# A threshold moved to ScalarE, value products regrouped, and gMLP one step later, in an attention and gMLP kernel

## The chip, the cores and the metric

The kernel runs on one core of a Trainium2 chip. The time is device microseconds of one execution. The kernel before was run three times: 563.73, 563.22 and 558.63 us, median 563.22. A further execution was recorded by the hardware profiler: its own time is 562.84 us, and the span from its first to its last instruction is 561.1 us. All rows of the profile come from that execution.

The engines are named as the profile names them: PE (TensorE, matmuls; PEld its weight loads), DVE (VectorE), ACT (ScalarE), POOL (GpSimd) and SP (SyncE, which here only issues DMAs). An issue queue has a q behind its name: SPq.

## The reference

For 8 batches of 8 heads, 576 positions and 64 values per head, each row of scores is thresholded: what lies more than tau (0.02) under the row's maximum is dropped before the softmax. The joined heads then go through a gMLP block, in which `w_spatial` mixes positions.

```python
scores = scale * np.matmul(q, k.transpose(0, 1, 3, 2))
thresh = np.max(scores, axis=-1, keepdims=True) - tau
scores = np.where(scores >= thresh, scores, -1000000000.0)
scores = scores - np.max(scores, axis=-1, keepdims=True)
attn = np.exp(scores)
attn = attn / (np.sum(attn, axis=-1, keepdims=True) + 1e-09)
x = np.matmul(attn, v)                      # heads joined: (8, 576, 512)

h = np.maximum(x @ w_in, 0.0)
u, v = h[..., :512], h[..., 512:]
v_n = (v - mean(v)) / np.sqrt(var(v) + 1e-06)          # over the last axis
v_s = np.einsum('ts,bsd->btd', w_spatial, v_n) + b_spatial[None, :, None]
out = (u * v_s) @ w_out
```

## The kernel before

**Pairs and steps.** Two heads of a batch make a pair; there are 32 pairs, four to a batch. The 576 query rows of a pair are cut into four chunks of 128 for each head and one remainder chunk, in which the last 64 rows of both heads share the 128 partitions. A step handles one chunk: step `g` is pair `g // 5`, chunk `c = g % 5`. So a batch is 20 steps, and the pairs are 160 steps. The order of all instructions is written out by hand: every engine works through its own instructions in program order, and DMAs go out in program order on the queue that issues them, nearly all on SP's.

**A step** (`step`, line 478) issues, in this order: the score matmuls of its chunk into one of two score tiles in PSUM (`scores`, lines 445 and 448); evictions held over from the step before; the first of up to two jobs; the row maximum on DVE, negated (`negm`, line 491); the eviction of the first job, if DVE does it; `e = exp(s - max)` on ACT, one activation per head (line 499); then `mask`, for the chunk of the step before; then what stands in the list `sends`; then second parts of the v jobs; then the second job. Jobs that ACT evicts come ahead of those that DVE evicts. If the second job is one that ACT evicts, its eviction is held until the next step begins. Jobs write to two one-bank tiles in PSUM, named f, in turn.

**mask** (line 459) makes `p = e * (e >= exp(-tau))` on DVE. Chunks 0 and 1 share a tile, as do 2 and 3; after the second of the two, one DMA on SP's queue transposes both into `pT`. The remainder chunk has its own, smaller operation (`pr`, line 473) and its own transpose into `ptr` (line 476). Since `mask` runs a step late, the remainder's is issued in step 0 of the next pair.

**Value products** (`pv`, line 251) of a pair run in steps 3 and 4 of the next pair, one head each: for each of five chunks, five matmuls of 65 columns add up over the keys. The 65th column of the value tile is one, so it gives the row sum. DVE evicts with a reciprocal (line 274) and a multiply (line 275) into `xn`. After the second head, the transpose of `xn` into `xT` is put into `sends`, which SP issues (line 281); with four of them the batch is ready for gMLP.

**gMLP jobs.** Each batch has 20: five each of v (line 308; relu on ACT at line 333, a square with a sum on ACT at line 341, the normalizing on POOL), u (lines 359 and 364; relu on ACT), s (lines 389 and 394, the product with `w_spatial`; DVE multiplies by u into `gT`) and o (line 418, the product with `w_out`; ACT copies, SP sends it out). `ORDER` gives the job of each of the 20 steps that begin 27 steps after the batch's first step; an `o` there belongs to the batch before. In the first three steps of a pair, the other job transposes the next pair's q and k on PE (lines 226 and 239), with a copy by ACT. What falls behind the last pair's steps is in a list of its own (`last`).

**w_spatial.** Between steps 23 and 35 POOL casts its five row chunks (`shape_ws`, line 182), each followed at once by a transposing DMA on SP's queue into `wsT` (line 189). In step 37, three small DMAs put the bias rows into the same tile (line 202).

Of the kernel before, what the change touches and what calls it, by code (L numbers as in the profile page):

```python
# [8 lines left out]
F32 = mybir.dt.float32  # L9
BF16 = mybir.dt.bfloat16  # L10
AX = mybir.AxisListType
ALU = mybir.AluOpType
ACT = mybir.ActivationFunctionType
# [4 lines left out]
def kernel(  # L18
# [16 lines left out]
    nc = tc.nc  # L35
    B, H, S, D = q.shape
# [5 lines left out]
    P = 128  # L42
# [5 lines left out]
    small = ctx.enter_context(tc.tile_pool(name="small", bufs=6))  # L48
# [11 lines left out]
    ctau = const.tile([P, 1], F32, name="ctau")  # L60
# [4 lines left out]
    pr_ring = [const.tile([P, 640], BF16, name=f"pr{i}") for i in range(2)]  # L65
# [34 lines left out]
    wsT = const.tile([P, 5, 640], BF16, name="wsT")  # L100
    wsb = const.tile([P, 5, 640], BF16, name="wsb")


    def load(i, n, w, eng=nc.sync):

        b, hp = divmod(i, HP)
        t = ld_ring[i // 2 % 2][w][:, 2 * (i % 2):2 * (i % 2) + 2 * n]
        src = (q, k, v)[w][b, 2 * hp:2 * hp + 2 * n]

        def main():  # L110
            eng.dma_start(
                out=t[:, :, 0:4, :],
                in_=src[:, 0:512, :].rearrange("h (p c) d -> p h (c d)", c=4))

        def rest():
            eng.dma_start(out=t[0:64, :, 4, :],
                          in_=src[:, 512:576, :].rearrange("h p d -> p h d"))

        def rest_b():
            nc.sync.dma_start(  # L120
                out=vx_ring[i // 2 % 2][64:128],
                in_=src.rearrange("(j h) s d -> h s j d", h=2)[1, 512:576])
        return [main, rest] + ([rest_b] if w == 2 else [])
# [32 lines left out]
    bias = mw.tile([P, 2, S], F32, name="gT")  # L156
# [25 lines left out]
    def shape_ws(c):  # L182
        n = P if c < 4 else 64
        src = wsl[c // 2][:n, c % 2, :]
        nc.gpsimd.tensor_copy(
            out=wsb[:n, c, 0:512].rearrange("p (sc sp) -> p sc sp", sc=4),
            in_=src[:, 0:512].rearrange("p (sp sc) -> p sc sp", sc=4))
        nc.gpsimd.tensor_copy(out=wsb[:n, c, 512:576], in_=src[:, 512:576])
        nc.sync.dma_start_transpose(out=wsT[:, :, c * P:(c + 1) * P], in_=wsb[:, c, :])

    def shape_bias(_):

# [14 lines left out]
    def bank():  # L207

        banks[0] += 1
        if "scores" in done_with and banks[0] % 2:  # L210
            return ps_s.tile([P, 1536], F32, name="s")[:, 0:512]
        return ps_f.tile([P, 512], F32, name="f")

    done_with = set()
    sends = []
    qks, pts, xns, xts = {}, {}, {}, {}

    def qk_main(i, which):
# [29 lines left out]
            nc.gpsimd.tensor_copy(out=kd[64:128, 64:128], in_=qks[i][64:128, 1, 512:576])  # L248
        return "act", mm, ev

    def pv(i, h):
        b, hp = divmod(i, HP)
        hold = {}
        vt = v_ring[i % 4]

        def mm():
            t = hold["t"] = bank()
            for c in range(5):
                for j in range(5):
                    if c < 4:  # L260
                        lhs = pts[i, c // 2][:, c % 2, 4 + (j + 1) % 5 if h else j, :]
                        rhs = vt[:, (10 if j == 4 else 5 + j) if h else j, :]
                    else:
                        lhs = pts[i, 2][:, j, 64 * h:64 * h + P]
                        rhs = vt[:, 5 * h + j, :]
                    nc.tensor.matmul(out=t[:, c * 65:c * 65 + 65], lhsT=lhs, rhs=rhs,  # L266
                                     start=(j == 0), stop=(j == 4))

        def ev():
            o = hold["t"][:, 0:325].rearrange("p (c d) -> p c d", d=65)  # L270
            if h == 0:
                xns[i] = xp.tile([P, 5, P], BF16, name="xn")
            r = small.tile([P, 5], F32, name="r")
            nc.vector.reciprocal(out=r, in_=o[:, :, 64])
            nc.vector.tensor_tensor(out=xns[i][:, :, h * D:(h + 1) * D], in0=o[:, :, 0:64],  # L275
                                    in1=r.unsqueeze(2).broadcast_to([P, 5, 64]), op=ALU.mult)
            if h == 1:
                if hp == 0:
                    xts[b] = xtp.tile([P, 4, 640], BF16, name="xT")
                xn = xns[i]  # L280
                sends.append(lambda: nc.sync.dma_start_transpose(
                    out=xts[b][:, hp, :].rearrange("p (c s) -> p c s", s=P),
                    in_=xn.rearrange("p c d -> p (c d)")))
        return "dve", mm, ev

    us, gs = {}, {}
# [149 lines left out]
    def scores(i, c):  # L436


        s = ps_s.tile([P, 1536], F32, name="s")
        qk = qks[i]  # L440

        def mm(h, out, lo, n):
            hs = slice(64 * h, 64 * h + 64)
            m = slice(c * P, min((c + 1) * P, S))
            return nc.tensor.matmul(out=out, lhsT=qk[hs, 0, m], rhs=qk[hs, 1, lo:lo + n],  # L445
                                    start=True, stop=True)
        if c < 4:
            nc.tensor.matmul(out=view(s, 512, [[448, 2], [1, 64]]),  # L448
                             lhsT=qk[:, 0, c * P:(c + 1) * P], rhs=kd_ring[i % 2],
                             start=True, stop=True)  # L450
            mm(0, s[:, 0:512], 0, 512)
            mm(1, s[:, 1024:1536], 0, 512)
            return view(s, 0, [[960, 2], [1, S]])
        for lo, off in ((0, 224), (288, 512)):
            for h in range(2):
                mm(h, s[64 * h:64 * h + 64, off:off + 288], lo, 288)
        return s[:, 224:800].rearrange("p (h s) -> p h s", h=1)

    def mask():
        i, c, e = unmasked.pop()  # L460
        if c < 4:
            pt = p_ring[c // 2]
            ef = e.rearrange("p h s -> p (h s)")
            nc.vector.scalar_tensor_tensor(out=pt[:, c % 2, :], in0=ef, scalar=ctau, in1=ef,  # L464
                                           op0=ALU.is_ge, op1=ALU.mult)
            if c % 2:
                dst = ptp.tile([P, 2, 9, P], BF16, name="pT")
                nc.sync.dma_start_transpose(out=dst.rearrange("p c b s -> p (c b) s"),
                                            in_=pt.rearrange("p c s -> p (c s)"))
                pts[i, c // 2] = dst  # L470
        else:
            pt = pr_ring[i % 2]
            nc.vector.scalar_tensor_tensor(out=pt[:, 0:S], in0=e[:, 0, :], scalar=ctau,  # L473
                                           in1=e[:, 0, :], op0=ALU.is_ge, op1=ALU.mult)
            pts[i, 2] = ptr_ring[i % 3]
            nc.sync.dma_start_transpose(out=pts[i, 2][:, :, 0:P], in_=pt)

    def step(i, c, f1, f2):

        if i is not None:  # L480
            s = scores(i, c)
        while held:
            held.pop(0)()
        if f1:
            f1[1]()
            if f1[0] == "act":
                f1[2]()
        if i is not None:
            nh = 2 if c < 4 else 1
            nm = small.tile([P, 2], F32, name="negm")  # L490
            nc.vector.tensor_reduce(out=nm[:, 0:nh], in_=s, axis=AX.X, op=ALU.max, negate=True)  # L491
        if f1 and f1[0] == "dve":
            f1[2]()
        due = [f for n, f in later if n <= 0]
        later[:] = [(n - 1, f) for n, f in later if n > 0]
        if i is not None:
            e = ep.tile([P, 2, S], F32, name="e")
            for h in range(nh):
                nc.scalar.activation(out=e[:, h, :], in_=s[:, h, :], func=ACT.Exp,  # L499
                                     bias=nm[:, h:h + 1])  # L500
        ready = sends[:]
        sends.clear()
        if unmasked:
            mask()
        for f in ready:
            f()
        if i is not None:
            unmasked.append((i, c, e))
        for f in due:
            f()  # L510
        if f2:
            f2[1]()
            if f2[0] == "dve":
                f2[2]()
            else:
                held.append(f2[2])
# [7 lines left out]


    LAG = 27
    ORDER = "vuvvuvuvuu" + "oososososs"
    jobs = {}
    for b in range(B - 1):
        n = dict.fromkeys("vuso", 0)  # L530
        for j, t in enumerate(ORDER):
            f = {"v": moe_v, "u": moe_u, "s": moe_s, "o": moe_o}[t]
# [11 lines left out]
    with tc.manual_schedule():  # L544
# [23 lines left out]
        for g in range(5 * NPAIR + (len(last) + 1) // 2):  # L568
            slot, c = divmod(g, 5)
            i = slot if slot < NPAIR else None  # L570
# [65 lines left out]
```

## Time and profile before

| | us |
|---|---|
| median of three runs | 563.22 (558.63 to 563.73) |
| profiled execution | 562.84 |
| its span | 561.1 |
| PE busy in the span | 487.0 (87%) |
| DVE busy | 470.5 (84%) |
| ACT busy | 328.2 (59%) |
| POOL busy | 240.8 (43%) |
| granted TensorE clock, mean | 0.959 |

Busy times are sums over instructions and can lie beside each other. In a row of instruction groups come line, engine and operation, output and inputs, the shapes, the count, then busy us and the mean ns of one, then the engine's idle time just before them and what ended it. In a timeline row come the start, the duration, the engine, the line and the operation; a bracket gives the idle time before it and what released it. The granted clock is that of TensorE, in parts of full speed.

### The profile page before, as it was taken

The numbers are of one execution on the slowest core, as the hardware profiler recorded it, in microseconds if no ns is written. First come the engines' busy times: TensorE is split into PE (matmuls) and PEld (weight loads), VectorE is DVE, ScalarE is ACT, GpSimd is POOL, SyncE is SP. The second block draws the span as 40 slices with busy tenths as digits, with TensorE's granted clock in tenths as the row PEclk, the third lists the DMA queues.
The fourth block names the chain that finished last, engine by engine and source line by source line (L and its number), as shares of the span: only waits on it lengthen the run. The fifth ranks groups of instructions, "written<-read, shape, count | busy, mean of one in ns | idle before, by whom it ended". The sixth has DMA issues, their size and how long they took to land.

```text
span 561.1 us, 10240 instructions
## 1 busy us (share of the span) xinstructions
PE 487.0 (87%) x3848; PEld 257.7 (46%) x3848; DVE 470.5 (84%) x535; ACT 328.2 (59%) x609; POOL 240.8 (43%) x413
## 2 busy tenths in 40 slices
PE   6774887987898999899879999889989999989886
PEld 4342443544354555455435554445444554545433
DVE  3894988997898899889968999889987899989553
ACT  2553454774467755676546765677555766677241
POOL 5426622685407732377204752178303762064020
PEclk9896888997999999999999999999998999999989
DMA  8599797985987888968997698978987588755822
GB/s 235 107 214 185 140 207 134 217 146 125 208 173 158 180 182 184 195 94 224 166 174 145 127 217 150 189 141 165 205 187 157 98 198 188 119 107 102 192 65 84
DMA packets 243601, 90.91 MB, mean 162 GB/s; under 512 B 213024, under 2 KB 238112, under 8 KB 243552
## 3 DMA queue, kind: packets, MB, share of 16 engines
q1 hardware_dynamic: 241936, 88.39, 76.9%
q0 software_dynamic: 1200, 1.58, 2.3%
q8 instruction: 30, 0.49, 0.4%
q10 hardware_dynamic: 416, 0.30, 0.2%
q14 instruction: 19, 0.16, 0.1%
HBM read 33.31 MB, written 9.44 MB: 76 GB/s over the span
## 4 chain that ended last, share of the span: by engine, by line
PE 47%; DVE 24%; DMA 12%; ACT 10%; issue 5%; SPq 1%; POOL 0%; ACTq 0%; POOLq 0%
PE s L445 18%; DVE negm L491 14%; PE f L266 7%; DVE p L464 7%; DMA ptr<-pr 7%; ACT e L499 5%; PE f L389 4%; DMA xT<-xn 4%; PE s L448 3%; PE f L359 3%; PE f L308 3%; PE f L418 3%; ACT sq L341 2%; DVE xn L275 1%; ACT vrel L333 1%
## 5 line engine op out<-in xcount | busy, mean ns | idle before, releaser
L499 ACT ACTIVATE e<-s,negm 128x576 f32<-128x576 f32 x288 | 199.5, 740 | 96.8 <-DVE negm L491 77.4
L491 DVE TENSOR_REDUCE negm<-s 128x2 f32<-128x1152 f32 (+1 forms) x160 | 197.2, 1233 | 47.3 <-PE s L445 45.9
L445 PE MATMUL s<-qkT 64*128 64x512 f32 (+1 forms) x768 | 191.1, 590 | 1.0 <-ACT e L499 1.0
L464 DVE SCALAR_TENSOR_TENSOR p<-e,ctau 128x1152 bf16<-128x1152 f32 x128 | 187.5, 1465 | 0.0
L445 PEld LDWEIGHTS s<-qkT 64*128 64x128 f32 (+1 forms) x768 | 55.6, 173 | 29.2 <-issue 2.8
L247 POOL COPY kd<-qkT 64x64 f32<-64x64 f32 x32 | 13.0, 406 | 129.4 <-ACT qkT L243 124.7
L230 ACT COPY qkT<-f 128x512 f32<-128x512 f32 x64 | 37.6, 588 | 50.1 <-PE f L226 50.1
L266 PEld LDWEIGHTS <-pT 128*128 128x128 bf16 x1280 | 49.1, 100 | 37.4 <-issue 25.8
L448 PE MATMUL s<-kd,qkT 128*128 128x128 f32 x256 | 55.4, 299 | 8.5 <-ACT e L499 5.5
L266 PE MATMUL f<-v,pT 128*128 128x65 bf16 x1260 | 53.1, 197 | 9.0 <-ACT vrel L333 4.6
L448 PEld LDWEIGHTS s<-kd,qkT 128*128 128x128 f32 x256 | 45.5, 197 | 21.8 <-ACT e L499 8.8
L308 PE MATMUL f<-w_in,xT 128*128 128x512 bf16 x140 | 37.8, 387 | 11.0 <-DMA xT<-xn 9.5
L142 POOL COPY kn<-kl 128x640 f32<-128x640 f32 x32 | 26.1, 817 | 32.8 <-DMA kl<-in_k_dram 20.3
L389 PE MATMUL f<-wsT,vn 128*128 128x512 bf16 x150 | 38.0, 384 | 2.1 <-ACT o L426 1.6
L335 POOL TENSOR_SCALAR nmean<-sm 128x1 f32<-128x1 f32 x35 | 11.8, 338 | 64.8 <-ACT vrel L333 64.8
L266 PE MATMUL f<-v,ptr 128*128 128x65 bf16 x315 | 21.2, 199 | 19.2 <-DMA ptr<-pr 19.2
L359 PE MATMUL f<-xT,w_in 128*128 128x512 bf16 x120 | 32.6, 396 | 5.8 <-ACT vrel L333 5.8
L139 POOL TENSOR_SCALAR qn<-ql 128x640 f32<-128x640 f32 x32 | 30.5, 953 | 11.6 <-DMA ql<-in_q_dram 10.7
L418 PE MATMUL f<-w_o,gT 128*128 128x512 bf16 (+1 forms) x128 | 33.8, 388 | 0.5
L333 ACT ACTIVATE vrel<-f 128x512 f32<-128x512 f32 x35 | 20.8, 595 | 20.8 <-PE f L308 20.8
L275 DVE TENSOR_TENSOR xn<-f,r 128x320 bf16<-128x320 f32 x63 | 31.0, 491 | 2.2
L473 DVE SCALAR_TENSOR_TENSOR pr<-e,ctau 128x576 bf16<-128x576 f32 x32 | 31.9, 997 | 0.0
(101 smaller groups left out, 530.5 us busy)
## 6 DMA issues: line engine op xcount, KB each, us to landing
vl<-in_v_dram SPq DMA_DIRECT2D x16, 512.0 KB, 4.7
out_dram<-o SPq DMA_DIRECT2D x32, 256.0 KB, 2.7
ql<-in_q_dram SPq DMA_DIRECT2D x15, 512.0 KB, 4.5
kl<-in_k_dram SPq DMA_DIRECT2D x15, 512.0 KB, 4.6
uT<-in_moe_w_spatial_dram SPq DMA_DIRECT2D x2, 576.0 KB, 5.1
vl<-in_v_dram SPq DMA_DIRECT2D x16, 64.0 KB, 2.8
pT<-p SPq DMA_TRANSPOSE x64, 5.5
w_in<-in_moe_w_in_dram POOLq DMA_DIRECT2D x4, 256.0 KB, 5.7
```

The lines of the kernel that those rows point to most:

```text
L230: nc.scalar.copy(out=qks[i][:, which, 0:512], in_=hold["t"])
L266: nc.tensor.matmul(out=t[:, c * 65:c * 65 + 65], lhsT=lhs, rhs=rhs, start=(j == 0), stop=(j == 4))
L275: nc.vector.tensor_tensor(out=xns[i][:, :, h * D:(h + 1) * D], in0=o[:, :, 0:64], in1=r.unsqueeze(2).broadcast_to([P, 5, 64]), op=ALU.mult)
L308: nc.tensor.matmul(out=t, lhsT=xts[b][:, f, c * P:(c + 1) * P], rhs=w_in[:, f, 512:1024], start=(f == 0), stop=(f == 3))
L359: nc.tensor.matmul(out=t, lhsT=w_in[:, m, f * P:(f + 1) * P], rhs=xts[b][:, m, 0:512], start=(m == 0), stop=(m == 3))
L389: nc.tensor.matmul(out=t, lhsT=vn[:, c, f * P:(f + 1) * P], rhs=wsT[:, c, 0:512], start=(c == 0), stop=(c == 4))
L418: nc.tensor.matmul(out=t[:n], lhsT=gs[b][:, f, c * P:c * P + n], rhs=w_o[:, f, :], start=(f == 0), stop=(f == 3))
L445: return nc.tensor.matmul(out=out, lhsT=qk[hs, 0, m], rhs=qk[hs, 1, lo:lo + n], start=True, stop=True)
L448: nc.tensor.matmul(out=view(s, 512, [[448, 2], [1, 64]]), lhsT=qk[:, 0, c * P:(c + 1) * P], rhs=kd_ring[i % 2], start=True, stop=True)
L464: nc.vector.scalar_tensor_tensor(out=pt[:, c % 2, :], in0=ef, scalar=ctau, in1=ef, op0=ALU.is_ge, op1=ALU.mult)
L491: nc.vector.tensor_reduce(out=nm[:, 0:nh], in_=s, axis=AX.X, op=ALU.max, negate=True)
L499: nc.scalar.activation(out=e[:, h, :], in_=s[:, h, :], func=ACT.Exp, bias=nm[:, h:h + 1])
```

## The change

Four edits:

- The remainder chunk's threshold leaves DVE. In step c = 4, DVE adds tau to the negated maximum (one column). ACT then applies a parametric ReLU to `score - max + tau`: values from 0 on pass, values below are multiplied by 1e30. A second activation takes the exponential, written straight into the tile that is transposed. Dropped values become zero, kept ones lie between 1 and exp(tau); the common factor goes out with the row sum. The multiply with comparison in `mask` is gone for this chunk; the transpose is issued where it was.
- The value products are cut by chunks instead of heads: step 3 has chunks 0 and 1 of both heads, step 4 has chunks 2, 3 and the remainder of both.
- In `ORDER` the v and u jobs come one step later, and the first o of the batch before stands ahead of them. The s jobs and the other o jobs keep their places.
- The transposing send of each `w_spatial` chunk is put into `sends` twice over: the step's list only puts the real send into the list of the next step.

```diff
@@ shape_ws
-        nc.sync.dma_start_transpose(out=wsT[:, :, c * P:(c + 1) * P], in_=wsb[:, c, :])
+        sends.append(lambda: sends.append(lambda: nc.sync.dma_start_transpose(
+            out=wsT[:, :, c * P:(c + 1) * P], in_=wsb[:, c, :])))
@@ pv
-    def pv(i, h):
+    def pv(i, part):
+
         b, hp = divmod(i, HP)
         hold = {}
         vt = v_ring[i % 4]
+        c0, c1 = ((0, 2), (2, 5))[part]
+        w = 2 * (c1 - c0)
 
         def mm():
             t = hold["t"] = bank()
-            for c in range(5):
-                for j in range(5):
...
-                    nc.tensor.matmul(out=t[:, c * 65:c * 65 + 65], lhsT=lhs, rhs=rhs,
-                                     start=(j == 0), stop=(j == 4))
+            for c in range(c0, c1):
+                for h in range(2):
+                    at = (2 * (c - c0) + h) * 65
+                    for j in range(5):
+                        if c < 4:
+                            lhs = pts[i, c // 2][:, c % 2, 4 + (j + 1) % 5 if h else j, :]
+                            rhs = vt[:, (10 if j == 4 else 5 + j) if h else j, :]
+                        else:
+                            lhs = pts[i, 2][:, j, 64 * h:64 * h + P]
+                            rhs = vt[:, 5 * h + j, :]
+                        nc.tensor.matmul(out=t[:, at:at + 65], lhsT=lhs, rhs=rhs,
+                                         start=(j == 0), stop=(j == 4))
 
         def ev():
-            o = hold["t"][:, 0:325].rearrange("p (c d) -> p c d", d=65)
-            if h == 0:
+            o = hold["t"][:, 0:65 * w].rearrange("p (g d) -> p g d", d=65)
+            if part == 0:
                 xns[i] = xp.tile([P, 5, P], BF16, name="xn")
-            r = small.tile([P, 5], F32, name="r")
-            nc.vector.reciprocal(out=r, in_=o[:, :, 64])
-            nc.vector.tensor_tensor(out=xns[i][:, :, h * D:(h + 1) * D], in0=o[:, :, 0:64],
-                                    in1=r.unsqueeze(2).broadcast_to([P, 5, 64]), op=ALU.mult)
-            if h == 1:
+            xn = xns[i]
+            r = small.tile([P, 6], F32, name="r")
+            nc.vector.reciprocal(out=r[:, 0:w], in_=o[:, :, 64])
+            nc.vector.tensor_tensor(
+                out=xn[:, c0:c1, :].rearrange("p c (h d) -> p (c h) d", h=2),
+                in0=o[:, :, 0:64], in1=r[:, 0:w].unsqueeze(2).broadcast_to([P, w, 64]),
+                op=ALU.mult)
+            if part == 1:
...
@@ mask
         else:
-            pt = pr_ring[i % 2]
-            nc.vector.scalar_tensor_tensor(out=pt[:, 0:S], in0=e[:, 0, :], scalar=ctau,
-                                           in1=e[:, 0, :], op0=ALU.is_ge, op1=ALU.mult)
             pts[i, 2] = ptr_ring[i % 3]
-            nc.sync.dma_start_transpose(out=pts[i, 2][:, :, 0:P], in_=pt)
+            nc.sync.dma_start_transpose(out=pts[i, 2][:, :, 0:P], in_=pr_ring[i % 2])
@@ step
             e = ep.tile([P, 2, S], F32, name="e")
-            for h in range(nh):
+            if c == 4:
+
+                nc.vector.tensor_scalar_add(out=nm[:, 0:1], in0=nm[:, 0:1], scalar1=float(tau))
+                nc.scalar.activation(out=e[:, 0, :], in_=s[:, 0, :], func=ACT.Prelu,
+                                     bias=nm[:, 0:1], alpha=1e30)
+                nc.scalar.activation(out=pr_ring[i % 2][:, 0:S], in_=e[:, 0, :], func=ACT.Exp)
+            for h in range(2 if c < 4 else 0):
                 nc.scalar.activation(out=e[:, h, :], in_=s[:, h, :], func=ACT.Exp,
                                      bias=nm[:, h:h + 1])
@@
     LAG = 27
-    ORDER = "vuvvuvuvuu" + "oososososs"
+    ORDER = "ovuvvuvuvuuososososs"
```

More of the change, by code (lines that the diff above doesn't have):

```diff
@@ L101 @@
     wsb = const.tile([P, 5, 640], BF16, name="wsb")
+    sends = []
     def load(i, n, w, eng=nc.sync):
@@ L214 @@
     done_with = set()
-    sends = []
     qks, pts, xns, xts = {}, {}, {}, {}
@@ L254, in pv @@
         vt = v_ring[i % 4]
+        c0, c1 = ((0, 2), (2, 5))[part]
+        w = 2 * (c1 - c0)
         def mm():
             t = hold["t"] = bank()
-            for c in range(5):
-                for j in range(5):
[L260 to L266, printed above, removed]
-                                     start=(j == 0), stop=(j == 4))
+            for c in range(c0, c1):
[10 more added lines that the diff above has]
+                                         start=(j == 0), stop=(j == 4))
@@ L277, in ev @@
-            if h == 1:
+            xn = xns[i]
[6 more added lines that the diff above has]
+            if part == 1:
                 if hp == 0:
                     xts[b] = xtp.tile([P, 4, 640], BF16, name="xT")
-                xn = xns[i]
```

## The prediction

> **What bounds the kernel now.** I read four views, coarse to fine: the page's engine shares and its chain, busy times by stretch, the list of waits, and the timeline where the waits lie.
>
> ```profile
> PE 487.0 (87%) x3848; PEld 257.7 (46%) x3848; DVE 470.5 (84%) x535; ACT 328.2 (59%) x609; POOL 240.8 (43%) x413
> ...
> PE 47%; DVE 24%; DMA 12%; ACT 10%; issue 5%; SPq 1%; POOL 0%; ACTq 0%; POOLq 0%
> ```
>
> PE and DVE are nearly equal, and the chain changes between them, with DMA and ACT in between. So I cut the span: the start, the first batch, then five batches of gMLP, each 20 steps (four head pairs), cut at the same step. Columns: window, length, busy time of PE, PEld, DVE, ACT, POOL, granted clock, DMA share, GB/s.
>
> ```profile
> 30.00:107.00 77.00, 58.52 (x459) 30.93 (x458) 64.10 (x68) 37.16 (x63) 32.86 (x48) 0.87 0.94 182
> 107.00:170.29 63.29, 53.99 (x454) 29.16 (x452) 56.09 (x59) 37.70 (x71) 32.26 (x54) 0.95 0.85 169
> 170.29:233.34 63.05, 57.65 (x483) 31.04 (x482) 57.16 (x62) 41.24 (x79) 28.53 (x50) 1.00 0.83 176
> 233.34:300.39 67.05, 59.25 (x483) 31.50 (x482) 57.90 (x63) 41.24 (x79) 28.68 (x50) 0.97 0.87 168
> 300.39:363.42 63.03, 57.65 (x483) 31.02 (x482) 57.05 (x62) 41.24 (x79) 28.27 (x50) 1.00 0.89 164
> 363.42:429.49 66.07, 60.57 (x482) 32.37 (x482) 57.70 (x63) 41.33 (x79) 28.59 (x50) 0.95 0.85 173
> 429.49:490.75 61.26, 57.67 (x483) 31.13 (x482) 56.87 (x62) 41.23 (x79) 28.28 (x50) 1.00 0.72 150
> 490.75:520.00 29.25, 27.09 (x227) 14.02 (x227) 27.07 (x31) 21.76 (x44) 15.99 (x30) 1.00 0.57 111
> ```
>
> At clock 1.00 a batch holds 57.65 us of PE work. The five whole batches from 170 on last 64.1 on average, the best 61.26. What lies above 57.65 is PE's waits, and 1.6 to 2.9 us more matmul time where the clock fell. The start, 30 to 107, has DMA at 0.94: there the transfers are the limit, not an engine. Now by pairs, in the same columns:
>
> ```profile
> 395.55:412.00 16.45, 15.69 (x119) 8.16 (x118) 15.83 (x18) 9.57 (x16) 4.30 (x7) 1.00 0.91 170
> 412.00:430.60 18.60, 16.08 (x124) 8.37 (x123) 13.35 (x17) 9.63 (x19) 1.12 (x5) 0.82 0.77 178
> 430.60:446.37 15.77, 14.29 (x113) 7.62 (x114) 13.85 (x14) 12.15 (x26) 11.47 (x22) 1.00 0.55 103
> 446.37:461.63 15.26, 14.53 (x129) 8.22 (x130) 14.35 (x16) 9.98 (x18) 11.13 (x17) 1.00 0.87 200
> 461.63:477.60 15.97, 15.18 (x117) 7.96 (x116) 15.35 (x18) 9.10 (x16) 4.55 (x7) 1.00 0.77 178
> 477.60:491.86 14.26, 13.69 (x126) 7.32 (x125) 13.64 (x17) 10.01 (x19) 1.45 (x5) 1.00 0.70 118
> ```
>
> Three kinds of pair. The pair of s and o jobs (first and fifth row) is DVE's: 15.83 of 16.45. The v and u pairs (third, fourth) are PE's with ACT in the way. The pair in which a batch's v jobs begin (second and last) takes 14.26 or 18.60. The waits say why; columns are waiter, releaser, total us, times, longest.
>
> ```profile
> PE f L266 <- DMA ptr<-pr: 19.2, 10, 6.1
> ...
> PE f L308 <- DMA xT<-xn: 9.5, 5, 3.4
> ...
> PE f L359 <- ACT vrel L333: 5.8, 7, 0.8
> ...
> PE f L364 <- ACT uT L374: 4.5, 6, 0.8
> ```
>
> **The change part by part.**
>
> *Remainder threshold on ScalarE.* The prices:
>
> ```profile
> L499 ACT ACTIVATE e<-s,negm 128x576 f32<-128x576 f32 x288 | 199.5, 740 | 96.8 <-DVE negm L491 77.4 <-DVE r L274 18.6
> ...
> L473 DVE SCALAR_TENSOR_TENSOR pr<-e,ctau 128x576 bf16<-128x576 f32 x32 | 31.9, 997 | 0.0
> ...
> L323 DVE TENSOR_SCALAR rs<-mv 128x1 f32<-128x1 f32 x5 | 0.8, 154 | 0.2
> ```
>
> DVE loses 32 of 0.997 us and gains 32 single-column adds; the nearest row is 0.154, so 0.84 is saved per pair, 27.0 us in all. ACT gains one activation per pair, at most 0.740 by the row with the same shape and a column bias: 23.7 us, to 352 of 561. On the path, step c=4 has one more hop: negm, add, Prelu, and only then is the score bank free, 0.15 us later than now. Where the value products are that step's first job, the add stands on DVE behind their eviction, so Prelu (and on ACT behind it the next step's q and k copies) waits for that; this is so before gMLP starts and in one pair per batch. Between nothing (that bank is next wanted two steps on) and the eviction's own 0.7, I put 0.3 us per batch.
>
> The 0.84 us counts where DVE is last: in the s/o pair, and there only down to PE's own 15.69 of 16.45 or 15.18 of 15.97, so at most 0.8; I take 0.6. In the v/u pairs it falls into DVE's idle time; there ACT goes from 12.15 to 12.9 of 15.77, still below. Does an earlier pr bring ptr earlier?
>
> ```profile
> 429.63 2.75 SPq L468 DMA_TRANSPOSE pT<-p  x1
> ...
> 432.44 0.62 SPq L116 DMA_DIRECT2D vl<-in_v_dram  x1
> ...
> 433.15 1.26 SPq L476 DMA_TRANSPOSE ptr<-pr  x1
> ```
>
> Hardly: SP's queue goes from the transpose of p to a load to ptr with 0.1 us between. DVE's pr is covered by SP itself, so I give this nothing.
>
> *Value products by chunk groups.* Still 50 matmuls, two reciprocals and two multiplies over 640 columns per pair; the pieces are 4 and 6 groups for 5 and 5, so the work is unchanged. What moves is the need. Now the first head at c=3 wants all five chunks; after, c=3 wants chunks 0 and 1 only, and ptr is wanted by the last ten matmuls of c=4, one step (15.77/5 = 3.15 us) later. The longest wait:
>
> ```profile
> 48.65 1.24 SPq L476 DMA_TRANSPOSE ptr<-pr  x1
> ...
> 55.14 0.46 PE L266 MATMUL f<-v,ptr 128*128 128x65 bf16 x5 [6.11 <-DMA ptr<-pr]
> ```
>
> Here PE and behind it DVE stood still, and the scores of c=4 and the threshold of the chunk before stood behind them. With the need one step later about 3 of 6.11 remain; the waits under 3.8 go. But this one lies where DMA is at 0.94: 0.94 of 77 is 72.4 us of transfers, so that stretch can't go below about 73. I give it 3 of its 77 (bounds 0 and 5).
>
> *w_spatial sends delayed.* In 107 to 170:
>
> ```profile
> 127.85 1.20 SPq L189 DMA_TRANSPOSE wsT<-wsb  x1
> ...
> 129.77 2.10 SPq L476 DMA_TRANSPOSE ptr<-pr  x1
> ...
> 134.44 0.45 PE L266 MATMUL f<-v,ptr 128*128 128x65 bf16 x5 [3.76 <-DMA ptr<-pr]
> ```
> ```profile
> SPq L189 <- POOL nm L346: 4.4, 1, 4.4
> ```
>
> SP stood 4.4 us for POOL's cast of w_spatial, with ptr and xT queued behind, and PE then 3.76 for ptr. Sent from the next step's list, the transpose comes behind ptr. New: the last one goes out a step before the bias rows are placed in the same tile, and SP waits for its landing there, some 1.5 us; nothing needs it for two steps. With the later need of ptr I give this window 4.5 of its 9.3 us idle (63.29 less 53.99); bounds 2 and 6.
>
> *gMLP one step later.* The v and u jobs move on by a step, and the first o of the batch before takes the vacated place; s and the other o jobs stay, the tail too. In the pair of 18.60:
>
> ```profile
> 415.89 1.34 SPq L281 DMA_TRANSPOSE xT<-xn  x1
> ...
> 420.02 0.61 PE L308 MATMUL f<-w_in,xT 128*128 128x512 bf16 x1 [2.30 <-DMA xT<-xn]
> ```
>
> xT arrives at 420.0; v asked at 420.02 less 2.30, 417.7. After, PE does the o matmuls there (they need the last gT, as v's bank does now) and next step's scores first, so it asks about 2.5 us later: waits up to 3.4 shrink to under 1. With the wait goes the slow clock behind it: 16.08 of PE for 124 matmuls at 0.82, 13.69 for 126 at 1.00. The Trainium skill ("TensorE: Matmul & The Clock Gate", Part 1) says that the clock halves after an idle window of about 3.4 us; taken literally a wait of 2.30 would not do it, the clock loss would stay in two batches, and the sum would end near 540, inside the forecast's range. The trace shows the fall after the shorter wait, so by the row it goes with the wait.
>
> The moved v jobs also change who waits for ACT: in the v/u pairs the square stands on ACT ahead of the relu that frees PE's bank:
>
> ```profile
> 433.25 0.72 ACT L341 ACTIVATE sq<-vrel,nmean 128x512 bf16<-128x512 f32 x1
> ...
> 433.96 0.59 ACT L333 ACTIVATE vrel<-f 128x512 f32<-128x512 f32 x1
> ...
> 434.69 1.02 PE L359 MATMUL f<-xT,w_in 128*128 128x512 bf16 x4 [0.82 <-ACT vrel L333]
> ```
>
> The 5.8 and 4.5 us above are waits of this kind, 0.82 and less each. With v at c=0 and c=1 in a row, no square is due between, so I expect one or two of these waits per batch to go, 1.0 us (bounds 0 and 1.6). Against that, ACT has the relu of u, relu of v, square and Prelu close together at c=3 and c=4. The last v is one step nearer to the first s, still four steps off.
>
> **The sum**, against the profiled execution: 562.84 for a span of 561.1, the median of three being 563.22, so they are one. A batch: from 61.26, the best, in which xT hardly cost anything on PE, less 0.6 in the s/o pair, less 1.0 of ACT waits, plus 0.3 and 0.3 for Prelu's place and a leftover xT wait: 60.3. Five batches: 320.5 less 301.5 = 19. With 3 (start), 4.5 (first batch) and 1 (end, 490 to 520, as half a batch less its xT share), 27.5: 562.8 - 27.5 = 535.
>
> **The rivals.**
>
> *Transfers hold it.* Faster batches ask for the same bytes in less time: 0.85 of 64.1 is 54.5 us of DMA per batch, 0.90 at 60.3, and at 0.94 the start is already held by them. Then the ptr and xT waits shrink but pT takes their place, batches stop at 61.3 (14 saved), the first batch gives 2, the start nothing: 547. For: SP's back-to-back queue. Against: the best batch ran at 0.72.
>
> *No change.* The waits only change names, since PE, DVE and ACT release each other in turn: within 5.6 us of 562.8. The sum of three engines' waits speaks for it, the direct PE waits of 19.2 and 9.5 against.
>
> *Slower: Prelu's table.* Before, one table load serves everything:
>
> ```profile
> L552 ACT ACT_TABLE_LOAD x1 | 1.3, 1283 | 2.0 <-issue 2.0
> ```
>
> If Prelu isn't in the set that holds Exp, each pair pays two loads, 2.57 us, on ACT between negm and the next Exp: 12.9 + 2.6 = 15.5 of 15.77 in the v/u pairs, and everywhere a hole of about 2 us that the two score banks can't cover. 32 pairs by 2, less the 27.5: 600. It decides as soon as the activation count shows more than one load. For it: no Prelu is in this trace. Against: Exp, Relu, Square and Copy all run here on that one load. By the Trainium skill ("ScalarE: Activation LUTs", What ACT_TABLE_LOAD costs) a switch is about 2.66 us with its drain, which would leave holes of some 4.7 and make it near 690 by estimate; its section "Same chain, other wiring" even says that the slope by alpha can't be reached from a kernel. No row here shows either.
>
> *Slower without loads.* ACT's queue at c=3 and c=4 holds PE's two banks: if every gain in the batches is lost and each pair's 0.74 lies on the path, 562.8 + 23.7 less 7.5 (start and first batch) gives 579. ACT's 12.9 of 15.77 speaks against.
>
> **Chances.** Forecast 0.62 (526 to 543), transfers 0.22 (543 to 556), better than 526 0.04, no change 0.06, slower 0.06 (0.04 the table, 0.02 ACT). A measurement of this kernel can tell about 1% from nothing. So faster 0.87, same 0.07, slower 0.06. The range takes in the first two cases: 525 to 552.
>
> **What would show it.** One table load; 32 Prelu near 0.74 us; DVE busy near 444; the ptr wait of PE under 6 us and no row of L308 waiting over 1 us on xT; batches of 60 to 61 at clock 0.98 or more; SP no longer waiting at the wsT send. I am wrong if PE waits for pT or for ACT take more than half of what ptr and xT leave, or if the start grows shorter than its transfers.

## The result, and the profile after

The changed kernel takes 539.65 us (median of four, 536.43 to 541.14) against 563.28 for the kernel before: a ratio of 0.9591, with a 95% interval of 0.952 to 0.9661. Measured a second time, it was 536.83 (six runs), ratio 0.9536 (0.9498 to 0.9573); the two medians are 2.8 us apart, and smaller differences between medians are not read as effects here. The forecast was 535 with a range of 525 to 552. The profiled execution took 536.43, with a span of 534.7 us.

The page's engine shares and chain by engine, after:

```profile
PE 480.9 (90%) x3848; PEld 254.3 (48%) x3848; DVE 447.7 (84%) x535; ACT 350.5 (66%) x641; POOL 233.0 (44%) x413
...
DVE 35%; PE 35%; ACT 13%; issue 8%; DMA 7%; SPq 2%; POOL 0%; ACTq 0%; POOLq 0%; DVEq 0%
```

DMA fell from 12% to 7% of the chain, and PE shares the lead with DVE now. Where the time went is seen when both spans are cut at the row maximum of a pair's remainder chunk (step c = 4), which is the same place of the program in every kernel. After, the stretches are: the pairs before gMLP in two pieces, the first batch of gMLP, and five further batches. Columns as in the prediction. First the same first piece before:

```profile
37.06:89.20 52.14, 37.27 (x278) 19.76 (x277) 40.83 (x43) 22.65 (x36) 24.83 (x34) 0.84 0.97 180
```
```profile
36.68:82.35 45.67, 33.61 (x278) 17.90 (x277) 38.96 (x44) 24.18 (x39) 25.97 (x33) 0.93 1.00 201
82.35:95.46 13.11, 10.20 (x67) 4.72 (x66) 12.54 (x15) 8.43 (x15) 2.91 (x7) 1.00 0.87 153
95.46:159.99 64.53, 58.12 (x467) 30.83 (x466) 54.54 (x62) 42.24 (x79) 33.53 (x57) 0.95 0.91 175
159.99:220.72 60.73, 57.98 (x481) 30.95 (x479) 54.54 (x62) 44.17 (x82) 26.68 (x49) 1.00 0.86 186
220.72:281.57 60.85, 58.15 (x482) 31.16 (x481) 54.63 (x62) 44.17 (x82) 27.96 (x49) 1.00 0.89 179
281.57:342.31 60.74, 58.03 (x482) 31.13 (x480) 54.55 (x62) 44.19 (x82) 27.59 (x49) 1.00 0.86 180
342.31:403.06 60.75, 57.94 (x481) 30.95 (x479) 54.56 (x63) 44.18 (x82) 26.61 (x49) 1.00 0.88 180
403.06:463.97 60.91, 58.21 (x483) 31.22 (x481) 54.62 (x62) 44.16 (x82) 26.92 (x49) 1.00 0.78 164
```

The five batches are now alike, 60.8 us each, at a clock of 1.00, where they had been 61.60 to 66.70 in this cut. The table has the same cut in every kernel's profiled execution (the changed kernel twice). The start is the two pieces before gMLP together. The kernels other than the first two are those of the experiments below.

| us | products by | job order | start | first batch | five batches |
|---|---|---|---|---|---|
| before | heads | old | 66.6 | 64.9 | 320.6 |
| changed | chunks | new | 58.8, 60.1 | 64.5, 63.5 | 304.0, 304.9 |
| job order alone | heads | new | 64.7 | 63.8 | 301.9 |
| chunk groups alone | chunks | old | 60.7 | 61.3 | 318.4 |
| threshold on ScalarE alone | heads | old | 66.1 | 68.0 | 319.6 |
| delayed sends alone | heads | old | 69.0 | 65.8 | 317.8 |
| changed, old job order | chunks | old | 61.8 | 62.2 | 322.4 |
| changed, products by heads | heads | new | 69.9 | 67.0 | 302.4 |
| changed, threshold on DVE | chunks | new | 60.1 | 65.2 | 302.6 |
| changed, undelayed sends | chunks | new | 60.4 | 60.9 | 304.8 |
| job order and chunk groups | chunks | new | 60.8 | 63.2 | 305.3 |
| changed, tau at once, earlier casts | chunks | new | 59.6 | 60.8 | 303.6 |
| changed, undelayed sends, tau at once | chunks | new | 60.2 | 63.1 | 305.1 |

Two columns fall into two groups each. The start goes by how the products are cut: 64.7 to 69.9 by heads, 58.8 to 61.8 by chunks. The five batches go by the job order: 317.8 to 322.4 with the old one, 301.9 to 305.3 with the new one. The first batch goes by neither.

So of the 26.4 us between the two profiled executions, 7.8 come from the start, 0.3 from the first batch, 16.6 from the five batches and the rest from the end. The waits after:

```profile
PE f L273 <- DMA ptr<-pr: 7.1, 3, 5.3
...
PE f L398 <- DMA wsT<-parts: 3.4, 1, 3.4
...
PE f L273 <- ACT uT L385: 3.0, 5, 0.6
PE f L273 <- ACT uT L383: 2.9, 7, 0.4
...
PE f L317 <- DMA xT<-xn: 1.3, 1, 1.3
```

PE's waits for ptr went from 19.2 to 7.1, for xT from 9.5 to 1.3. The waits of 5.8 and 4.5 for ACT's relus are gone, with 5.9 of new ones in the rows of L273. And there is a wait that was not there: 3.4 us for the bias rows.

### The profile page after: what moved, and what is told of

Same layout as the page of the kernel before. It is cut to its first block, busy times and chain, and to the rows that moved or that the text cites. A ratio compares the mean times of both kernels' runs of the same rounds, so it can differ in the third digit from the quotient of the medians.

```text
span 534.7 us, 10265 instructions
## 1 busy us (share of the span) xinstructions
PE 480.9 (90%) x3848; PEld 254.3 (48%) x3848; DVE 447.7 (84%) x535; ACT 350.5 (66%) x641; POOL 233.0 (44%) x413
## 4 chain that ended last, share of the span: by engine, by line
DVE 35%; PE 35%; ACT 13%; issue 8%; DMA 7%; SPq 2%; POOL 0%; ACTq 0%; POOLq 0%; DVEq 0%
DVE negm L497 17%; PE s L454 13%; DVE p L473 13%; ACT e L511 8%; PE f L273 6%; PE f L398 3%; PE f L368 3%; PE s L457 3%; DMA ptr<-pr 2%; DVE xn L283 2%; PE f L228 2%; DMA pT<-p 2%; ACT sq L350 2%; PE f L317 2%; DVE gT L412 1%
## 5 line engine op out<-in xcount | busy, mean ns | idle before, releaser
L473 DVE SCALAR_TENSOR_TENSOR p<-e,ctau 128x1152 bf16<-128x1152 f32 x128 | 190.3, 1487 | 1.5 <-DMA pT<-p 1.1
L454 PE MATMUL s<-qkT 64*128 64x512 f32 (+1 forms) x768 | 187.2, 578 | 3.3 <-ACT e L511 3.3
L273 PEld LDWEIGHTS <-pT 128*128 128x128 bf16 x1280 | 47.3, 98 | 33.8 <-issue 28.0
L249 POOL COPY kd<-qkT 64x64 f32<-64x64 f32 x32 | 7.4, 231 | 121.3 <-ACT qkT L245 120.7
L273 PE MATMUL f<-v,pT 128*128 128x65 bf16 x1260 | 50.5, 194 | 8.1 <-ACT uT L385 3.0
L144 POOL COPY kn<-kl 128x640 f32<-128x640 f32 x32 | 39.0, 1219 | 23.3 <-DMA kl<-in_k_dram 21.2
L352 POOL TENSOR_SCALAR rs<-ss 128x1 f32<-128x1 f32 x35 | 6.7, 192 | 60.7 <-ACT sq L350 60.0
L283 DVE TENSOR_TENSOR xn<-f,r 128x256 bf16<-128x256 f32 (+1 forms) x63 | 30.9, 490 | 2.2
L141 POOL TENSOR_SCALAR qn<-ql 128x640 f32<-128x640 f32 x32 | 25.1, 785 | 8.8 <-DMA ql<-in_q_dram 7.2
L356 POOL TENSOR_SCALAR vn<-vrel,rs,nm 128x512 bf16<-128x512 f32 (+1 forms) x35 | 27.0, 771 | 3.8
L228 PEld LDWEIGHTS f<-identf,qn 128*128 128x128 f32 x128 | 14.9, 152 | 28.0 <-ACT pr L509 13.6
```

Of the source, the lines that this page charges most:

```text
L144: nc.gpsimd.tensor_copy(out=t, in_=src)
L273: nc.tensor.matmul(out=t[:, at:at + 65], lhsT=lhs, rhs=rhs, start=(j == 0), stop=(j == 4))
L283: nc.vector.tensor_tensor(out=xn[:, c0:c1, :].rearrange("p c (h d) -> p (c h) d", h=2), in0=o[:, :, 0:64], in1=r[:, 0:w].unsqueeze(2).broa ...
```

## The experiments

First each edit alone, put into the kernel before; then the changed kernel without each.

**Job order alone.**

```diff
-    ORDER = "vuvvuvuvuu" + "oososososs"
+    ORDER = "ovuvvuvuvuuososososs"
```

> The kernel before with the new order of the gMLP jobs alone. Theory (each edit takes away its own wait): the waits of v on xT go, with the slow clock behind them, and some waits of PE for ACT: five batches from 64.1 to 60.5-61.5 us, 13 to 18 us saved, about 547 us. Rival (one cause behind all waits: the remainder's late transpose also holds up xT on SP's queue): the wait moves to ptr and less than 7 us is saved, above 556 us.

Measured: 541.27 us, ratio 0.9603 (0.9534 to 0.9673). This one line gives most of the gain, more than the theory's 547. Its batches, and its wait on xT:

```profile
166.12:226.17 60.05, 57.45 (x475) 31.03 (x481) 57.08 (x62) 41.34 (x78) 29.37 (x49) 1.00 0.86 181
226.17:286.23 60.06, 57.20 (x473) 30.92 (x479) 57.07 (x62) 41.30 (x78) 28.99 (x49) 1.00 0.92 182
```
```profile
PE f L308 <- DMA xT<-xn: 1.8, 3, 1.3
```

The five batches take 60.4 on average, a little less than the 60.8 of the full change. The rival falls: ptr still cost PE 17.6 us here, and the gain came all the same.

**Chunk groups alone** (the `pv` part of the diff).

> The kernel before with the value products cut by chunk groups alone. Theory: PE's waits for ptr (19.2 us in all) shrink to a third, 5 to 8 us in the start, up to 4 in the first batch, 1 to 3 in the batches: about 553 us. The waits of v on xT stay. Rival (transfers hold the start): 560 us or more, PE waiting for pT in place of ptr.

Measured: 552.53, ratio 0.982 (0.9737 to 0.9902), as the theory had it. In the start the DMA share is 1.01, and PE's wait for ptr is 7.2, down from 19.2; the wait on xT stays at 8.9:

```profile
37.55:84.17 46.62, 34.74 (x276) 18.36 (x276) 41.51 (x44) 22.57 (x36) 24.05 (x31) 0.89 1.01 193
```
```profile
PE f L315 <- DMA xT<-xn: 8.9, 5, 2.9
...
PE f L271 <- DMA ptr<-pr: 7.2, 3, 5.0
```

**The threshold on ScalarE alone** (the `mask` and `step` parts of the diff).

> The kernel before with the remainder's threshold on ScalarE alone. Theory: 0.6 us saved in the one pair per batch that DVE bounds, 0.3 lost in another, something in the pairs before gMLP starts: 559 to 562 us. Rival 1 (DVE's 27 us are on the path): 545 to 553. Rival 2 (the add behind the evictions and ACT's longer queue cost more than DVE saves): 564 to 570.

Measured: 563.58, ratio 1.0028 (0.9991 to 1.0065): no difference. It misses the theory's gain of 1 to 4 us. The first rival falls; of the second, a loss of up to 3.7 us lies inside the interval, so a small cost is not excluded. DVE is busy 23 us less (447.5 for 470.5), and the time is no shorter, so that work was not on the path. The pair behind the first s job, cut as above, shows why: it takes 16.06 us before and 16.06 here. DVE's wait for the scores in it grows by 0.73 us, about what the threshold took there (0.81). First the kernel before, then this one:

```profile
204.92 1.36 DVE L491 TENSOR_REDUCE negm<-s 128x2 f32<-128x1152 f32 x1 [0.41 <-PE s L445]
```
```profile
207.73 1.36 DVE L488 TENSOR_REDUCE negm<-s 128x2 f32<-128x1152 f32 x1 [1.14 <-PE s L445]
```

**Delayed w_spatial sends alone** (the `shape_ws` part).

> The kernel before with the delayed w_spatial sends alone. Theory: SP no longer stands 4.4 us for POOL, PE's wait of 3.76 us for ptr in the first batch goes, 2 to 5 us saved: 558 to 561. Rival (a new wait takes its place: the first s job for the bias rows, which wait for the last of these transposes): no change, 562 to 565, with PE waiting 2 us or more on the bias rows.

Measured: 563.55, ratio 1.0023 (0.9981 to 1.0064). The rival holds: no difference, and PE waits 2.2 us for the bias rows. SP's standing only moved: 6.5 us at these sends before (4.4, 1.2 and 0.9), here 3.3 at the sends and 3.2 at the bias rows behind them.

```profile
PE f L390 <- DMA wsT<-parts: 2.2, 1, 2.2
```

**The changed kernel with the old job order.**

```diff
-    ORDER = "ovuvvuvuvuuososososs"
+    ORDER = "vuvvuvuvuu" + "oososososs"
```

> The changed kernel with the old order of the gMLP jobs. Theory (own waits): the waits on xT return in some batches, 8 to 14 us slower than the changed kernel's 539.65, 548 to 553. Rival (the other edits bring xT early enough by themselves): within 4 us of it.

Measured: 554.82, ratio 0.985 (0.9817 to 0.9884), a little above the theory's range. The waits on xT are back, larger than before (13.5 for 9.5), and with them the clock below 1.00 in three of the five batches, of which the second is one:

```profile
161.05:224.28 63.23, 57.69 (x482) 31.07 (x481) 53.89 (x63) 44.09 (x82) 28.04 (x49) 1.00 0.89 185
224.28:290.53 66.25, 59.93 (x480) 31.95 (x478) 54.05 (x62) 44.08 (x82) 28.10 (x49) 0.95 0.85 174
```
```profile
PE f L317 <- DMA xT<-xn: 13.5, 7, 3.5
```

**The changed kernel with products by heads** (the `pv` part undone).

> The changed kernel with value products by heads again. Theory: waits for ptr return, mostly in the start and the first batch, 5 to 10 us slower, 545 to 550; the pair of s and o jobs gets 0.5 us shorter, as its larger second part is gone. Rival: within 3 us.

Measured: 545.24, ratio 0.9683 (0.9635 to 0.9731), within the theory's range. Start and first batch carry it (table above), and the pair after the first s job is 0.7 us shorter, 16.29 for 16.98. Not all of the 69.9 and 67.0 need be the heads' doing: the order alone, by heads too, has 64.7 and 63.8.

**The changed kernel with the threshold on DVE.**

> The changed kernel with the remainder's threshold on DVE again. In its profile the pair that begins with the first s is 16.98 us, 0.9 longer than before, and the add stands behind the evictions there. Theory now: taken alone this edit gains about nothing in the batches, since what it saves in other pairs it loses there: 538 to 542. Rival (what was predicted, and the start's gain is this edit's): 543 to 548.

Measured: 535.5, ratio 0.9502 (0.9469 to 0.9536). That is below the theory's range and not to be told from the 0.9536 of the changed kernel's second measurement. The rival falls. The batches are 60.3 to 61.2 long and the pair in question 16.45.

**The changed kernel with undelayed sends.**

> The changed kernel with the w_spatial sends undelayed. Its profile shows PE waiting 3.4 us on the bias rows in the first batch, which gained only 0.3 us in all. Theory now: undelayed sends take that wait away and bring back SP's stand for POOL, whose price the later need of ptr now hides: 2 to 4 us faster, 535 to 538. Rival (as predicted, the delay helps): 541 to 545.

Measured: 535.53, ratio 0.9501 (0.9464 to 0.9538), at the theory's figure; its first batch is 60.9 for 64.5 and 63.5. Against the second measurement of the changed kernel the whole time is no certain gain.

**The changed kernel, a second time,** measured beside the three that follow.

> The changed kernel once more, beside the next three on one chip. 536 to 541 us; batches of 60.7 to 60.9 us, the pair after the first s job 16.98.

Measured: 536.83, ratio 0.9536 (0.9498 to 0.9573).

**Job order and chunk groups, without the other two edits.**

> The kernel before with the new job order and the value products by chunk groups, and neither the ScalarE threshold nor the delayed sends. Theory (those two edits as written cost about 4 us each): 530 to 535, batches of 60.2, the first batch near 61. Rival (the two costs seen are the scatter of the start, where the transfers are the limit): 536 to 541, as the changed kernel beside it.

Measured: 534.5, ratio 0.9504 (0.9462 to 0.9546). The total is in the theory's range, but its reason is not borne out: the first batch is 63.2 and not 61, the batches 60.8 and up, and the pair after the first s job takes 17.03 us without any work moved to ScalarE. The two edits left out together change nothing in the total that can be told from the scatter.

**Tau added at once, and earlier casts,** in the changed kernel.

```diff
             nc.vector.tensor_reduce(out=nm[:, 0:nh], in_=s, axis=AX.X, op=ALU.max, negate=True)
+            if c == 4:
+                nc.vector.tensor_scalar_add(out=nm[:, 0:1], in0=nm[:, 0:1], scalar1=float(tau))
...
-                nc.vector.tensor_scalar_add(out=nm[:, 0:1], in0=nm[:, 0:1], scalar1=float(tau))
...
-    for n, g0, d, f in ((4, 6, 4, load_w_in), (3, 8, 4, load_ws), (5, 23, 3, shape_ws),
+    for n, g0, d, f in ((4, 6, 4, load_w_in), (3, 8, 4, load_ws), (5, 20, 3, shape_ws),
```

> The changed kernel with two mendings, which show in different stretches: tau is added right behind the row maximum, ahead of the value products' eviction, and POOL's casts of w_spatial begin at step 20 instead of 23. Theory: the multiply with comparison again starts before POOL's copy of q in the pair after the first s job and takes 1.41 instead of 1.94 us, that pair 16.45 instead of 16.98, batches 60.2; the wait of PE on the bias rows is gone and the first batch's third pair falls from 21.0 to below 18: 532 to 536 in all. Rival for the pair (the larger second part on DVE is what makes it long): 16.9, batches 60.7. Rival for the first batch (SP's queue is full there, whatever waits): above 20.

Measured: 532.34, ratio 0.9463 (0.9427 to 0.9499): the fastest of all, and beside it on the same chip the changed kernel was at 0.9498 to 0.9573, so the two intervals only just meet. The part on the first batch holds. No wait on the bias rows is left, its third pair takes 14.9 us for 21.0, and the stretch is as short as the others:

```profile
96.64:157.42 60.78, 55.34 (x457) 29.78 (x464) 54.07 (x62) 42.04 (x78) 34.45 (x55) 0.97 0.96 190
157.42:218.14 60.72, 57.59 (x474) 31.12 (x480) 54.72 (x62) 44.12 (x82) 26.77 (x49) 1.00 0.80 178
```

The part on the pair falls. The add now comes ahead of the eviction, and p still takes 1.99 us, the pair 16.97:

```profile
248.41 0.15 DVE L499 TENSOR_SCALAR negm<-negm 128x1 f32<-128x1 f32 x1
...
249.37 1.99 DVE L473 SCALAR_TENSOR_TENSOR p<-e,ctau 128x1152 bf16<-128x1152 f32 x1
...
249.44 0.72 POOL L141 TENSOR_SCALAR qn<-ql 128x640 f32<-128x640 f32 x1
```

**Undelayed sends, with tau added at once.**

> The changed kernel with undelayed w_spatial sends and tau added right behind the row maximum. Theory: as the two edits alone or up to 2 us better, since what ScalarE takes over then costs nothing and saves in the pairs before gMLP starts: 530 to 534. Rival (the threshold on ScalarE costs by ACT's longer queue, wherever the add stands): 2 to 4 us above the two edits.

Measured: 534.87, ratio 0.9484 (0.9442 to 0.9527), beside the two edits' 534.5: the same. The longer queue of ScalarE costs nothing that can be measured, and the threshold there brings nothing. Its first batch is 63.1, though its sends are undelayed, with 0.6 us of waiting on the bias rows.

## Why the prediction was right, and where it was not

*gMLP one step later* was the largest term, and is the one that is shown best: in the five batches 18.6 us alone, and the loss of all of it when it alone is undone. Both halves of the step are there. The waits on xT went, and with them the slow clock: each of the five batches of the changed kernel is at 1.00. The waits for ACT's relus fell from 14.9 (5.8, 4.5 and 4.6 for the value products) to 5.9, over seven batches 1.3 us each, where 1.0 was forecast; against that, PE's waits for DVE's gT rose by 3 us in all. The sum for a batch was 60.3 and it is 60.8; 16.6 saved in place of 19. The row of before that the prediction doesn't show:

```profile
PE f L266 <- ACT vrel L333: 4.6, 7, 0.7
```

The step that failed in this term is "0.6 in the s/o pair". That pair got longer, from 16.06 to 16.98, so it came out 1.5 us worse than forecast, and the rest of the batch came out about 1 us better. The work left DVE in step 0, where DVE waits for the scores anyway (0.41 us before, 1.14 without the threshold). What lengthens the pair is the new order: it makes it 16.29 by itself. With the chunk groups added, whose second part puts 64 columns more on DVE in step 4, ahead of the next p, it is 16.45 or 17.0, depending on one meeting of DVE with POOL, told below. With the old order the chunk groups leave it at 16.05, alone and in the changed kernel. Neither the place of the add nor the threshold on ScalarE decides it: 17.03 without either.

*The start* was forecast at 3, within 0 and 5, and gave 7.8. The step that failed is "0.94 of 77 is 72.4 us of transfers, so that stretch can't go below about 73". In the cut used here, the first piece before had a DMA share of 0.97 over 52.14 us, 50.6 us; after, 1.00 over 45.67, 45.7 us, at 201 GB/s for 180. The bytes are nearly the same, 9.2 and 9.4 MB; the busy time is not a fixed amount of work. So one of the prediction's signs of being wrong came: the start is 58.8 us long, where the transfers before were 62.6 (0.94 of 66.6). A term is also missing. Of the 6.5 us that the first piece lost, 3.7 are matmul time: the same 278 records take 33.61 us at a clock of 0.93 for 37.27 at 0.84. The prediction counted the clock in the batches alone. The longest wait itself went as the working had it, only less far. ptr is wanted 1.5 us behind its issue for 0.4 before, not a step of 3.15 later, and it is still late:

```profile
47.13 2.51 SPq L482 DMA_TRANSPOSE ptr<-pr  x1
...
53.96 0.73 PE L273 MATMUL f<-v,ptr 128*128 128x65 bf16 x10 [5.32 <-DMA ptr<-pr]
```

5.32 of 6.11 remain, not 3; but what stood behind it, the scores of c = 4 and the threshold of the chunk before, now runs ahead of it. That the shorter start is the chunk groups' doing is shown by the two groups in the table's column.

*The first batch* was forecast at 4.5, within 2 and 6, and gave 0.3. The failed step is the sentence on the sends: "SP waits for its landing there, some 1.5 us; nothing needs it for two steps". The wait is near the forecast, 1.9 us (3.1 the second time), but the first s job two steps on does need the rows, in its last matmul:

```profile
SPq L205 <- DMA wsT<-wsb: 1.9, 1, 1.9
...
SPq L191 <- POOL rs L354: 2.7, 2, 1.4
...
SPq L191 <- POOL nm L355: 2.1, 2, 1.0
```
```profile
127.41 1.88 SPq L205 DMA_DIRECT2D wsT<-parts  x3
...
130.49 0.58 PE L398 MATMUL f<-wsT,vn 128*128 128x512 bf16 x1 [3.37 <-DMA wsT<-parts]
```

SP issues the rows at 127.4, PE stands until 130.5, and in the 4.6 us after that the granted clock is 0.50. While it stands, from 127.1 to 130.4, the DMA share is 0.02, so bandwidth is not what it waits for. Nor did the delay free SP: its one stand of 4.4 us went, but in all it stands 4.8 us at the delayed sends and 1.9 at the bias rows, for 6.5 before. Earlier casts end PE's wait. The price shows in one pair: where the new order and the chunk groups are both in, the third pair of the first batch takes 20.1 to 21.0 us with delayed sends, 15.6 to 17.4 with undelayed ones, and 14.9 with earlier casts. The pair behind it makes up for a part, so for the whole first batch the difference is less sure: 63.5 to 65.2 with the delay, 60.9 to 63.2 without it.

*The threshold on ScalarE* was priced right piece by piece. Activations and the add, and the one table load:

```profile
L507 ACT ACTIVATE e<-s,negm 128x576 f32<-128x576 f32 x32 | 23.7, 740 | 34.2 <-DVE negm L506 34.2
...
L509 ACT ACTIVATE pr<-e 128x576 bf16<-128x576 f32 x32 | 21.9, 684 | 1.0
...
L506 DVE TENSOR_SCALAR negm<-negm 128x1 f32<-128x1 f32 x32 | 4.8, 150 | 0.7
...
L564 ACT ACT_TABLE_LOAD x1 | 1.3, 1283 | 2.0 <-issue 2.0
```

One load means that the rival of 600 us did not occur: Prelu and Exp ran here without a second load. The Trainium skill's "ScalarE: Activation LUTs" says under "Same chain, other wiring" that the slope by alpha can't be reached from a kernel; this kernel sets it to 1e30, and its dropped values come out as zero only by that slope. DVE ended at 447.7 for 443.5 worked out, ACT at 350.5 for 352. But its worth in the sum, a net of 1.5 us, is not there: alone the ratio is 1.0028.

The sum of 27.5 stands against 26.4 between the profiled executions, and against 23.6 and 26.0 between medians. It is right to that degree by luck: a start that gave 4.8 more than forecast makes up for a first batch that gave 4.2 less and batches that gave 2.4 less. On the tell-tales: ptr at 7.1 missed "under 6", xT's longest wait of 1.3 missed "over 1" by little, and SP still waits at the wsT send. In the rival on transfers, "0.85 of 64.1" is a little high: its five rows average 0.83, which makes 0.89 at 60.3. The sentence that draws on the Trainium skill ("TensorE: Matmul & The Clock Gate", Part 1) gave 540 from the rule taken literally, and the first median is 539.65; that agreement is chance, as none of the five batches kept the slow clock.

## What to carry to other kernels

When PE waits on a transfer once in many steps, look at what is wanted first of it, and move that one job by one step or put its need last within a job; here that was worth more than taking 23 us of work off a busy engine. Before moving work from one engine to another, ask in which step the busy engine is last. Work taken from a step in which it has slack was worth nothing (the pair stayed at 16.06), and 0.59 us more in a step in which it had none made the pair 0.58 longer. A DMA that is sent later to unblock a queue needs its own reader checked, and the reader's reader.

## What the runs showed of the hardware

The multiply with comparison (p, two inputs in SBUF) and POOL's scaling of q hold each other up. In the pair after the first s job, p and POOL's scaling of q start within 0.07 us of each other, and it is either the one or the other that is stretched. First the kernel with two edits, then the changed kernel with the threshold on DVE:

```profile
252.81 2.00 DVE L471 SCALAR_TENSOR_TENSOR p<-e,ctau 128x1152 bf16<-128x1152 f32 x1
252.88 0.72 POOL L139 TENSOR_SCALAR qn<-ql 128x640 f32<-128x640 f32 x1
```
```profile
254.44 1.41 DVE L473 SCALAR_TENSOR_TENSOR p<-e,ctau 128x1152 bf16<-128x1152 f32 x1
254.51 1.91 POOL L141 TENSOR_SCALAR qn<-ql 128x640 f32<-128x640 f32 x1
```

Either p takes 2.00 and qn 0.72, or p 1.41 and qn 1.91. The recorded starts stand in the same order both times, so they don't tell who wins, and the pair is 17.03 or 16.45 us accordingly. Within a kernel it goes the same way in that pair of each of the five batches. What decides it was not found. The meeting itself comes with the new job order: in the kernel before, POOL scales q at 197.38, ahead of this pair, and p at 200.50 takes 1.41. The Trainium skill ("SBUF — State Buffer", "SBUF: two separate sides") says that VectorE, with two inputs in SBUF, and GpSimd contend for one pair of ports, and that one has it for a whole instruction while the other is blocked. The durations agree in the main: p is 0.59 us longer where qn takes 0.72, and qn 1.19 longer where p takes 1.41, so most of the other's length, though not all of it.

A wait of PE cost clock as well as its own time, but not in proportion: the prediction's windows of the kernel before show 1.00 in a batch with a single wait on xT of 2.0 us, 0.95 in one with 2.3, and 0.97 in one with 3.4.
